# Fewer key loads per head, one load for the reciprocals, maxima written straight into the queries' rows, and other planned landing times

## Chip, core and metric

The kernel runs on one core of a Trainium2 chip. The time is that of one execution on the device in microseconds (us), lower is better. TensorE (PE) multiplies matrices, VectorE (DVE), ScalarE (ACT) and GpSimd (POOL) work elementwise, and SyncE (SP) issues all DMAs of this kernel, in the order of its program.

## What is computed

Two independent parts stand side by side in the output, 2048 rows of 2 x 448 columns, all in float32:

```
a = real part of a 2D discrete Fourier transform of A_x[2048, 448], by matrix products:
    y = Cr @ (x @ Wre^T) - Ci @ (x @ Wim^T)
qkv = B_x[2048, 448] @ wqkv[448, 1344]          # 16 heads, 28 wide
p = softmax(q @ k^T / sqrt(28))                 # per head 2048 x 2048
b = concat_heads(p @ v) @ wo[448, 448]
out = concat([a, b], axis=-1)
```

B_x, wqkv and wo are scaled up by 8, so that the scores are large and the maxima have to be subtracted before the exponential.

## The kernel before

**A planner writes the order.** Nothing in the program is scheduled on the chip: each engine runs its instructions in program order and waits on semaphores. The kernel first collects tasks (`pe`, `act`, `dve`, `pool`, `dma`), each with a key (when it is wanted), dependencies, buffers and a planned duration, and `Schedule.run` then plays an event simulation of its own: whenever an engine is free in the plan, it takes the ready task with the smallest key and emits its instructions. For a DMA the plan takes an issue time of about 0.38 us on SP and a landing time worked out from a size in KB and an `extra` in us; at most `LANES` = 8 DMAs are in flight, and a further one waits for the eighth before it. Where the chip is later than the plan, an engine stands at the early instruction, and all that is behind it in its queue stands too. Changing one planned number moves instructions on all engines.

**What TensorE runs.** Products of float32 precision are made of high and low parts in a rounded format (fp32r). First x @ wqkv: the projections of queries and keys (`project`, matmuls at L547) go to the DRAM tensor `qk_d`, two numbers (high, low) for each element, one row of 2048 columns per channel; the values (`values`) go to `v_d`. The Fourier part (`hidden` at L547, `sequence` at L662) is the filler: its keys are spread from the start to 1120, and it fills TensorE between the matmuls of attention.

**Attention.** A unit is a head h and a chunk c of 512 queries. 64 units run in two lanes side by side. In `unit_kept` (48 units, three a head) all scores of the chunk are made once (L803, 16 matmuls), copied to SBUF by ACT (L415), reduced to a running maximum `rm` on DVE (L813), whose transposes (L820, L829) give the maxima `nm` and `mb`; POOL or DVE subtract them (L846), ACT takes the exponential (L850), and the product with the values (L734) runs in groups of eight. In `unit_twice` (16 units, one a head) the scores are made twice: a first pass (L753) only for the maxima (L757, L761); the negated maxima are transposed (`max_rows`, L716), split into a high part (ACT, L765) and a low part (DVE, L766) and stored to the DRAM tensor `nm_d` (L769), and loaded from there into rows 84 and 85 of the queries' tile `q` (L770). There they meet two rows of ones below the keys (L374), so that the matmul of the second pass (L781, 86 rows) subtracts the maxima itself, and ACT takes the exponential straight from PSUM (L785). `due` holds the keys of both passes: the lane of `unit_twice` has a pace `P_R` of 60, its first pass starts at i x `P_R`, its second `ahead` = 1.08 paces later. So the second pass of head h - 2 ends a little after the first pass of head h is to start.

**Loads of a head.** `head_loads` takes one of the two key tiles `k` (84 rows x 2048) for a head: it becomes free when the second pass of the head before the last is done. It is filled by four pairs of DMAs, one pair for each 512 columns: `rows_of` loads the 28 high rows twice (L689, 56 rows) and the 28 low rows once (L690). A matmul waits only for the pair of its own columns (`got_k[h, c]`). The queries of a unit are loaded by the same helper (`load_q`), the values by one DMA (L706).

**Sums.** The values have a column of ones, so the product's row 28 is the sum of the exponentials. `out_of` handles the four chunks of a head together (for the last two heads: pairs of units, 4 groups of 2; 18 groups in all): a matmul folds the partial products (L865), ACT copies them to `osb` (L867), one DMA takes the rows of sums to a [128, 16] tile `sm` (L870), DVE takes the reciprocals (L871), one DMA stores them to DRAM (`rd`, L872), and a DMA for each of the units loads its row of 512 reciprocals to all 32 rows of the unit in `sbc` (L876, with a step of 0 in the source). POOL multiplies (L879), and a DMA for each unit stores 28 rows to `on_d` (L882). The last projection loads these rows (L939, L944), splits them (L956, L411) and multiplies by wo (L974).

Of the kernel before, what the change touches and what calls it, by code (L numbers as in the profile page):

```python
# [11 lines left out]
F32 = mybir.dt.float32  # L12
# [8 lines left out]
S = 2048  # L21
D = 448
H = 16
DH = 28
P = 128
NT = S // P
CH = 512
NC = S // CH
KR = 3 * DH
VW = 32  # L30
# [16 lines left out]
def f32(ap):  # L47
    return ap.bitcast(F32)
# [11 lines left out]
FIRST = {"PE": 1.4, "ACT": 2.0, "DVE": 2.0, "POOL": 5.0, "SP": 0.75}  # L60
FLOW_AT = 4.1
X_ROWS = 2.0
AHEAD = 0.15
PE_TURN = 0.22

# [251 lines left out]
def tile_kernel(ctx, tc, xa, wre, wim, wd, xb, wqkv, wo, out):  # L317
    nc = tc.nc
    ctx.enter_context(tc.manual_schedule(engines={ET.PE, ET.Activation, ET.DVE, ET.Pool, ET.SP}))
    dram = ctx.enter_context(tc.tile_pool(name="dram", bufs=1, space=DRAM))  # L320
# [11 lines left out]

    qk_d = dram.tile([2 * D, 2, S], F32R, name="qkd")
    v_d = dram.tile([H, P, NT * VW], F32, name="vd")
    nm_d = [dram.tile([2, CH], F32, name=f"nmd{u}") for u in range(H * NC)]
    r_d = [dram.tile([P, NT if h < H - 2 else NT // 2], F32, name=f"rd{h}") for h in range(H - 2 + NC)]
    y_d = [dram.tile([P, D], F32, name=f"yd{t}") for t in range(NT)]
    on_d = dram.tile([D, S], F32, name="ond")
# [56 lines left out]
    def dma(key, emit, size=256, extra=0.0, n=1, **kw):  # L395

        return sch.add({"SP": 0.4}, key, lambda e: emit(), dmas=[(size, extra)] * n, **kw)
# [24 lines left out]
    lane_r = [u for u in units if u[1] in TWICE[u[0]]]  # L422
    lane_k = [u for u in units if u[1] not in TWICE[u[0]]]
    P_R = (T_END - T_ATT) / (len(lane_r) + 1.5)
    P_K = (T_END - T_ATT) / (len(lane_k) + 1.5)
    due = {}
    for lane, per, ahead, part in ((lane_r, P_R, 1.08, 1.0), (lane_k, P_K, 1.8, 1.0)):
        for i, u in enumerate(lane):
            due[u] = (T_ATT + i * per, T_ATT + (i + ahead) * per, part * per / 16)
    head_due = [min(due[h, c][0] for c in range(NC)) for h in range(H)]  # L430
# [254 lines left out]
    def rows_of(dst, once, r0, c0, c1):  # L685

        src = bass.AP(tensor=qk_d.tensor, offset=qk_d.offset + r0 * 2 * S + c0,
                      ap=[[2 * S, DH], [0 if once else S, 2], [1, c1 - c0]])
        nc.sync.dma_start(f32(dst[:2 * DH, :]), f32(src))  # L689
        nc.sync.dma_start(f32(dst[2 * DH:KR, :]), f32(qk_d[r0:r0 + DH, once, c0:c1]))  # L690

    def rows_ready(h, c, at):
        r = h * 2 * DH + at
        return [t for j in range(r // P, (r + DH - 1) // P + 1) for t in qk_done[j, c]]

    KT, VT, Q = {}, {}, {}
    got_k, got_v = {}, {}

    def head_loads(h):
        k = KT[h] = kt_s.slot()  # L700
        for c in range(NC):
            got_k[h, c] = [dma(head_due[h] - 14 + c, lambda c=c: rows_of(
                k.t[:, c * CH:(c + 1) * CH], 1, h * 2 * DH + DH, c * CH, (c + 1) * CH),
                size=84, extra=X_ROWS, n=2, deps=rows_ready(h, c, DH), use=[k])]
        v = VT[h] = v_s.slot()
        got_v[h] = [dma(head_due_b[h] - 12, lambda: nc.sync.dma_start(  # L706
            v.t.rearrange("p c t d -> p (c t d)"), v_d[h]), deps=[d for c in range(NC) for d in v_done[c]], use=[v])]
# [34 lines left out]
    def unit_twice(u):  # L742
        h, c = u
        t_a, t_b, dt = due[u]
        q = qr_s.slot()
        lq = load_q(u, q)
        mx, nm = mx_s.slot(), nm_s.slot()
        ms = []
        for kc in range(NC):
            for qt in range(4):  # L750
                o = bank_s.slot()
                key = t_a + (kc * 4 + qt) * dt
                m = pe(key, lambda e, o=o, kc=kc, qt=qt: nc.tensor.matmul(  # L753
                    o.t, q.t[:KR, qt * P:(qt + 1) * P], KT[h].t[:KR, kc * CH:(kc + 1) * CH], start=True, stop=True),
                    deps=[*lq, *got_k[h, kc], before.get("ra")], use=[o, q, KT[h], mx])
                in_line("ra", m)
                ms.append(dve(key - 20, lambda o=o, kc=kc, qt=qt: nc.vector.tensor_reduce(  # L757
                    mx.t[:, qt, kc:kc + 1], o.t, axis=AX.X, op=ALU.max), deps=[m],
                    use=[o, mx]))
        key = t_a + 16 * dt - 20  # L760
        r = dve(key, lambda: nc.vector.tensor_reduce(nm.t, mx.t, axis=AX.X, op=ALU.max, negate=True), 0.2,  # L761
                deps=ms, acq=[nm], use=[mx])
        o, n2 = bank_s.slot(), n2_s.slot()
        t = max_rows(key, o, nm, r)
        a = act(key, lambda o=o: nc.scalar.activation(n2.t[:, 0, :], o.t[:4, :P], AF.Copy), 0.2, deps=[t], acq=[n2], use=[o])  # L765
        b = dve(key, lambda o=o: nc.vector.tensor_tensor(n2.t[:, 1, :], o.t[:4, :P], f32(n2.t[:, 0, :]), op=ALU.subtract), 0.25,  # L766
                deps=[a], use=[o, n2])
        nd = nm_d[h * NC + c]
        s = dma(key, lambda: nc.sync.dma_start(nd.rearrange("r (a b) -> a r b", a=4), f32(n2.t)), size=4, deps=[b], use=[n2])  # L769
        ld = dma(key, lambda: nc.sync.dma_start(f32(q.t)[KR:KR + 2, :], nd), size=4, deps=[s], use=[q])  # L770
        po = bank_s.slot()
        last_pv = None
        for g in range(NT // GV):
            tiles, es = [], []
            for kt in range(GV * g, GV * (g + 1)):
                o = bank_s.slot()
                if kt % 2 == 0:
                    tiles.append(kept_s.slot())
                p = Half(tiles[-1], kt % 2)
                key = t_b + kt * dt  # L780
                m = pe(key, lambda e, o=o, kt=kt: nc.tensor.matmul(  # L781
                    o.t, KT[h].t[:KR + 2, kt * P:(kt + 1) * P], q.t[:KR + 2, :], start=True, stop=True),
                    deps=[ld, before.get("rb")], use=[o, p.pair, q, KT[h], po])
                in_line("rb", m)
                es.append(act(key - 20, lambda o=o, p=p: nc.scalar.activation(p.t, o.t, AF.Exp, scale=SCALE),  # L785
                              deps=[m], use=[o, p.pair]))
            last_pv = pv_group(u, g, tiles, [*es, last_pv], po, key)
        unit_out(u, po, last_pv, key - 20)
# [67 lines left out]
    def out_of(us, rd):  # L856

        key = max(due[u][1] for u in us) + 10
        n = len(us)
        o, pair = bank_s.slot(), kept_s.slot()  # L860
        osb, sbc = Half(pair, 0), Half(pair, 1)

        def emit(e):
            for i, u in enumerate(us):
                nc.tensor.matmul(o.t[i * VW:(i + 1) * VW, :], fold, OU[u].t, start=True, stop=True)  # L865
        m = pe(key, emit, d=0.86, deps=[ou_done[u] for u in us], use=[o, *(OU[u] for u in us)], mode=1)
        a = act(key - 20, lambda: nc.scalar.activation(osb.t[:n * VW], o.t[:n * VW], AF.Copy), deps=[m], use=[o, pair])  # L867

        sm = sm_s.slot()
        s2 = dma(key, lambda: nc.sync.dma_start(sm.t[:, :n * NC], osb.t[DH:n * VW:VW, :]), 8, 0.7, deps=[a], use=[sm, pair])  # L870
        r = dve(key - 20, lambda: nc.vector.reciprocal(sm.t[:, :n * NC], sm.t[:, :n * NC]), 0.3, deps=[s2], use=[sm])  # L871
        s3 = dma(key, lambda: nc.sync.dma_start(rd, sm.t[:, :n * NC]), 8, deps=[r], use=[sm])  # L872

        def spread():
            for i in range(n):
                nc.sync.dma_start(sbc.t[i * VW:(i + 1) * VW, :], bass.AP(  # L876
                    tensor=rd.tensor, offset=rd.offset + i * CH, ap=[[0, VW], [1, CH]]))
        s4 = dma(key, spread, 64, n=n, deps=[s3], use=[pair])
        mul = pool(key - 20, lambda: nc.gpsimd.tensor_tensor(osb.t[:n * VW], osb.t[:n * VW], sbc.t[:n * VW], op=ALU.mult),  # L879
                   deps=[s4], use=[pair])  # L880
        for i, (h, c) in enumerate(us):
            o_done[h, c] = dma(key, lambda i=i, h=h, c=c: nc.sync.dma_start(  # L882
                on_d[h * DH:(h + 1) * DH, c * CH:(c + 1) * CH], osb.t[i * VW:i * VW + DH, :]), 56, deps=[mul], use=[pair])
# [21 lines left out]
    key = fkey(0, 0)  # L905
# [5 lines left out]
    key = fkey(0, 0)  # L911
# [19 lines left out]
    for n, c in enumerate(LAST):  # L931
        raws = []
        for k in range(4):
            pair = kept_s.slot()
            raw = Half(pair, 0)
            key = T_OUT + n
            deps = [o_done[h, c] for h in range(H) if (h + 1) * DH > k * P and h * DH < (k + 1) * P] + [before["ka"]]
            if k < 3:
                ld = dma(key, lambda raw=raw, k=k, c=c: nc.sync.dma_start(raw.t, on_d[k * P:(k + 1) * P, c * CH:(c + 1) * CH]),  # L939
                         deps=deps, use=[pair])  # L940
            else:
# [3 lines left out]
                ld = dma(key, twice, 128, n=2, deps=deps, use=[pair])  # L945
            raws.append((raw, ld))
        for i in range(2):
            x = kt_s.slot()
            ready = []
            for k in range(4):  # L950
                raw, ld = raws[k]
# [3 lines left out]
                key = T_OUT + n + i / 2  # L955
# [7 lines left out]
            for t in range(2):  # L963
# [12 lines left out]
                pair = kept_s.slot()  # L976
# [43 lines left out]
```

## Time and profile before

| | us |
|---|---|
| median of 3 runs | 1185.3 (1184.34 to 1186.82) |
| the profiled execution, its own time | 1186.24 |
| its span in the trace | 1184.5 |
| TensorE: time in L662 (big, whi), L803, L734, the costliest groups | 328.6, 292.0, 240.7 |
| POOL in the subtraction L846 | 626.9 |
| DVE in the running maximum L813 | 461.1 |
| ACT in copies L415 and exponentials L850 | 408.5, 395.1 |
| SP: wait for POOL at L515 (weight loads of the Fourier part), 77 times | 235.8 |

The granted TensorE clock is 0.997 of full speed over the span. The page of a profile gives each engine's busy time; idle time of an engine that isn't the bottleneck costs nothing by itself. Because matmuls overlap (one takes some 0.37 to 0.41 us and the next starts after 0.2), TensorE counts as busy through short waits. "Waited for" is told by the instruction that came last before the wait ended. SP's issues aren't counted as work of an engine, but they take time on SP: SPq is its queue. The prediction shows the lines that it reads.

### The profile page before, as it was taken

The numbers are of one execution on the slowest core, as the hardware profiler recorded it, in microseconds if no ns is written. First come the engines' busy times: TensorE is split into PE (matmuls) and PEld (weight loads), VectorE is DVE, ScalarE is ACT, GpSimd is POOL, SyncE is SP. The second block draws the span as 40 slices with busy tenths as digits, with TensorE's granted clock in tenths as the row PEclk, the third lists the DMA queues.
The fourth block names the chain that finished last, engine by engine and source line by source line (L and its number), as shares of the span: only waits on it lengthen the run. The fifth ranks groups of instructions, "written<-read, shape, count | busy, mean of one in ns | idle before, by whom it ended". The sixth has DMA issues, their size and how long they took to land.

```text
span 1184.5 us, 19835 instructions
## 1 busy us (share of the span) xinstructions
PE 1164.1 (98%) x6426; PEld 809.4 (68%) x6426; DVE 936.7 (79%) x1468; ACT 1056.5 (89%) x1777; POOL 909.9 (77%) x525
## 2 busy tenths in 40 slices
PE   8999999999999999999999999999999999999998
PEld 7876656666667666766666667666667676667677
DVE  6599988888888868877787888987877888877742
ACT  5279999999999989998899999999999999999942
POOL 1157868989888979877797989897987897997730
PEclk9999999999999999999999999999999999999999
DMA  7792235322323232323132232323232423223643
GB/s 244 165 225 107 100 124 174 90 81 62 106 68 110 62 109 67 105 72 90 62 102 89 78 118 67 106 64 111 83 99 89 121 76 115 87 62 100 188 130 119
DMA packets 111736, 125.18 MB, mean 106 GB/s; under 512 B 49264, under 2 KB 63216, under 8 KB 111632
## 3 DMA queue, kind: packets, MB, share of 16 engines
q1 hardware_dynamic: 111632, 123.91, 35.4%
q8 instruction: 51, 0.84, 0.3%
q14 instruction: 53, 0.43, 0.1%
HBM read 89.98 MB, written 33.75 MB: 104 GB/s over the span
## 4 chain that ended last, share of the span: by engine, by line
PE 82%; ACT 6%; DMA 4%; DVE 2%; issue 2%; POOL 2%; SPq 1%; ACTq 0%; POOLq 0%; DVEq 0%
PE bank L662 23%; PE bank L734 17%; PE bank L803 14%; PE bank L547 11%; PE bank L781 5%; PE bank L753 5%; PE bank L974 3%; ACT kept L415 3%; PE bank L820 2%; PE bank L829 2%; DVE rm L813 2%; ACT kept L850 1%; PE bank L865 1%; DMA kept<-xb 1%; POOL kept L846 1%
## 5 line engine op out<-in xcount | busy, mean ns | idle before, releaser
L846 POOL TENSOR_TENSOR kept<-kept,mb 128x1024 f32<-128x1024 f32 x263 | 626.9, 2404 | 124.0 <-ACT mb L831 101.4
L813 DVE TENSOR_TENSOR rm<-bank,rm 128x512 f32<-128x512 f32 x672 | 461.1, 686 | 74.9 <-ACT kept L415 33.5
L415 ACT ACTIVATE kept<-bank 128x512 f32<-128x512 f32 (+1 forms) x715 | 408.5, 633 | 53.9 <-PE bank L803 34.6
L850 ACT ACTIVATE kept<-kept 128x1024 f32<-128x1024 f32 x372 | 395.1, 1102 | 11.3 <-DVE kept L846 5.5
L662 PE MATMUL bank<-big,whi 128*128 128x448 f32 x1024 | 328.6, 370 | 0.0
L803 PE MATMUL bank<-qk,k 84*128 84x512 f32 x768 | 292.0, 410 | 2.7 <-ACT kept L415 1.4
L522 POOL TENSOR_TENSOR wlo<-wraw,whi 128x512 fp32r<-128x512 f32 (+1 forms) x166 | 204.0, 1232 | 70.3 <-ACT whi L516 46.7
L734 PE MATMUL bank<-kept,v 128*32 128x512 f32 x1988 | 240.7, 597 | 0.7 <-DVE rm L813 0.5
L662 PEld LDWEIGHTS bank<-big,whi 128*128 128x128 f32 x1024 | 193.7, 190 | 28.8 <-issue 3.5
L803 PEld LDWEIGHTS bank<-qk,k 84*128 84x128 f32 x768 | 141.9, 189 | 69.3 <-DVE rm L813 17.7
L662 PE MATMUL bank<-big,wlo 128*128 128x448 f32 x512 | 189.0, 369 | 0.0
L757 DVE TENSOR_REDUCE mx<-bank 128x1 f32<-128x512 f32 x256 | 173.3, 682 | 18.8 <-PE bank L753 18.0
L785 ACT ACTIVATE kept<-bank 128x512 f32<-128x512 f32 x250 | 157.6, 639 | 5.3 <-PE bank L781 5.0
L734 PEld LDWEIGHTS bank<-kept,v 128*32 128x32 f32 x1988 | 56.6, 109 | 124.0 <-issue 111.9
L846 DVE TENSOR_TENSOR kept<-kept,bank 128x1024 f32<-128x1024 f32 x109 | 131.8, 1212 | 2.6 <-ACT mb L831 2.4
L516 ACT ACTIVATE whi<-wraw 128x512 fp32r<-128x512 f32 x167 | 112.1, 673 | 17.0 <-DMA wraw<-wqkv 12.2
L781 PE MATMUL bank<-qr,k 86*128 86x512 f32 x256 | 104.3, 411 | 2.9 <-DMA qr<-nmd 2.2
L662 PEld LDWEIGHTS bank<-big,wlo 128*128 128x128 f32 x512 | 97.2, 190 | 13.7 <-issue 0.8
L753 PE MATMUL bank<-k,qr 84*128 84x512 f32 x256 | 103.5, 413 | 2.3 <-ACT kept L785 0.9
L547 PE MATMUL bank<-wd,whi 128*128 128x448 f32 x256 | 80.6, 368 | 0.1
L547 PE MATMUL bank<-big,whi 128*128 128x512 f32 x196 | 69.8, 400 | 2.0 <-ACT big L482 0.9
L822 DVE TENSOR_REDUCE nm<-bank 128x4 f32<-128x512 f32 x48 | 33.1, 690 | 46.5 <-PE bank L820 43.4
(80 smaller groups left out, 1062.0 us busy)
## 6 DMA issues: line engine op xcount, KB each, us to landing
wraw<-wre SPq DMA_DIRECT2D x64, 256.0 KB
wraw<-wim SPq DMA_DIRECT2D x64, 256.0 KB
qkd<-wd SPq DMA_DIRECT2D x32, 256.0 KB
wraw<-xa SPq DMA_DIRECT2D x32, 256.0 KB
k<-qkd SPq DMA_DIRECT2D x64, 112.0 KB
out<-kept SPq DMA_DIRECT2D x32, 224.0 KB
qkd<-kept SPq DMA_DIRECT2D x24, 256.0 KB
qk<-qkd SPq DMA_DIRECT2D x48, 112.0 KB
```

The lines of the kernel that those rows point to most:

```text
L415: nc.scalar.activation(dst, src, AF.Copy)
L522: b = sch.add(e, at, lambda g: eng[g].tensor_tensor(self.lo.t[:, :n], raw.t[:, :n], f32(self.hi.t)[:, :n], op=ALU.subtract), deps=[a], acq ...
L547: nc.tensor.matmul(o.t[:, :cols], w(), x(), start=(i == 0), stop=(i == n - 1))
L662: nc.tensor.matmul(o.t[:, :D], a.t[:, k, :], b[:, q * 4 + k, :], start=(q == 0 and k == 0 and j == 0), stop=(q == 3 and k == 3 and j == 2))
L734: nc.tensor.matmul(o.t[j * VW:(j + 1) * VW, :], VT[h].t[:, kt // 4, j, :], pairs[i // 2].t[:, i % 2, :], start=(kt < 4), stop=(kt >= NT - 4))
L753: m = pe(key, lambda e, o=o, kc=kc, qt=qt: nc.tensor.matmul(o.t, q.t[:KR, qt * P:(qt + 1) * P], KT[h].t[:KR, kc * CH:(kc + 1) * CH], start ...
L757: ms.append(dve(key - 20, lambda o=o, kc=kc, qt=qt: nc.vector.tensor_reduce(mx.t[:, qt, kc:kc + 1], o.t, axis=AX.X, op=ALU.max), deps=[m], ...
L781: m = pe(key, lambda e, o=o, kt=kt: nc.tensor.matmul(o.t, KT[h].t[:KR + 2, kt * P:(kt + 1) * P], q.t[:KR + 2, :], start=True, stop=True), ...
L803: m = pe(key, lambda e, o=o, kt=kt: nc.tensor.matmul(o.t, KT[h].t[:KR, kt * P:(kt + 1) * P], q.t[:KR, :], start=True, stop=True), deps=[*l ...
L813: prev = dve(key - 20, lambda o=o: nc.vector.tensor_tensor(rm.t, o.t, rm.t, op=ALU.max), deps=[m, prev], use=[rm, o], lock=[o], own=RAW)
L846: eng[e].tensor_tensor(s.t, s.t, over_pair(pm.t if e == "DVE" else mb.t), op=ALU.add)
L850: es.append(act(key, lambda s=s: nc.scalar.activation(s.t, s.t, AF.Exp, scale=SCALE), 0.96, deps=[sh], use=[s]))
```

## The change

1. A head's keys are loaded by one pair of DMAs for all 2048 columns, for heads 1 to 15; head 0 keeps its four pairs. All four `got_k[h, c]` are this one load, which waits until all four chunks of the projection are stored. Its planned `size` is 344 and its `extra` `X_K` = 2.0, for each of the two DMAs.
2. The negated maxima no longer go through DRAM (`nm_d` is gone): two DMAs, one for each of the high and low parts, take the [4, 128] values from `n2` to one row of 512 in the queries' tile. Planned `extra` `X_NM` = 0.3.
3. The reciprocals of a group are loaded by one DMA to all n x 32 rows (source: n chunks, each row 32 times by a step of 0, 512 columns), in place of n DMAs.
4. Planned landings in `out_of`: the sums' load has an `extra` of 3.0 in place of 0.7, the store and the load of the reciprocals 1.5 in place of 0.
5. `ahead` of the `unit_twice` lane is 1.04 in place of 1.08.

```diff
+X_K = 2.0
+X_NM = 0.3
...
-    nm_d = [dram.tile([2, CH], F32, name=f"nmd{u}") for u in range(H * NC)]
...
-    for lane, per, ahead, part in ((lane_r, P_R, 1.08, 1.0), (lane_k, P_K, 1.8, 1.0)):
+    for lane, per, ahead, part in ((lane_r, P_R, 1.04, 1.0), (lane_k, P_K, 1.8, 1.0)):
...
-        for c in range(NC):
-            got_k[h, c] = [dma(head_due[h] - 14 + c, lambda c=c: rows_of(
-                k.t[:, c * CH:(c + 1) * CH], 1, h * 2 * DH + DH, c * CH, (c + 1) * CH),
-                size=84, extra=X_ROWS, n=2, deps=rows_ready(h, c, DH), use=[k])]
+        if h == 0:
+            for c in range(NC):
+                got_k[h, c] = [dma(head_due[h] - 14 + c, lambda c=c: rows_of(
+                    k.t[:, c * CH:(c + 1) * CH], 1, h * 2 * DH + DH, c * CH, (c + 1) * CH),
+                    size=84, extra=X_ROWS, n=2, deps=rows_ready(h, c, DH), use=[k])]
+        else:
+            ld = dma(head_due[h] - 14, lambda: rows_of(k.t, 1, h * 2 * DH + DH, 0, S), size=344, extra=X_K, n=2,
+                     deps=[t for c in range(NC) for t in rows_ready(h, c, DH)], use=[k])
+            for c in range(NC):
+                got_k[h, c] = [ld]
...
-        nd = nm_d[h * NC + c]
-        s = dma(key, lambda: nc.sync.dma_start(nd.rearrange("r (a b) -> a r b", a=4), f32(n2.t)), size=4, deps=[b], use=[n2])
-        ld = dma(key, lambda: nc.sync.dma_start(f32(q.t)[KR:KR + 2, :], nd), size=4, deps=[s], use=[q])
+        def put():
+            for r in range(2):
+                nc.sync.dma_start(f32(q.t)[KR + r:KR + r + 1, :].rearrange("r (a b) -> r a b", a=4), f32(n2.t)[:, r, :])
+        ld = dma(key, put, size=2, extra=X_NM, n=2, deps=[b], use=[n2, q])
...
-        s2 = dma(key, lambda: nc.sync.dma_start(sm.t[:, :n * NC], osb.t[DH:n * VW:VW, :]), 8, 0.7, deps=[a], use=[sm, pair])
+        s2 = dma(key, lambda: nc.sync.dma_start(sm.t[:, :n * NC], osb.t[DH:n * VW:VW, :]), 8, 3.0, deps=[a], use=[sm, pair])
...
-        s3 = dma(key, lambda: nc.sync.dma_start(rd, sm.t[:, :n * NC]), 8, deps=[r], use=[sm])
-
-        def spread():
-            for i in range(n):
-                nc.sync.dma_start(sbc.t[i * VW:(i + 1) * VW, :], bass.AP(
-                    tensor=rd.tensor, offset=rd.offset + i * CH, ap=[[0, VW], [1, CH]]))
-        s4 = dma(key, spread, 64, n=n, deps=[s3], use=[pair])
+        s3 = dma(key, lambda: nc.sync.dma_start(rd, sm.t[:, :n * NC]), 8, 1.5, deps=[r], use=[sm])
+
+        s4 = dma(key, lambda: nc.sync.dma_start(sbc.t[:n * VW, :], bass.AP(
+            tensor=rd.tensor, offset=rd.offset, ap=[[CH, n], [0, VW], [1, CH]])), 64 * n, 1.5, deps=[s3], use=[pair])
```

## The prediction

> **What bounds the kernel now.** First the page's busy times, and the same for the middle stage (its length, then each engine's busy time and count, TensorE first).
>
> ```profile
> span 1184.5 us, 19835 instructions
> PE 1164.1 (98%) x6426; PEld 809.4 (68%) x6426; DVE 936.7 (79%) x1468; ACT 1056.5 (89%) x1777; POOL 909.9 (77%) x525
> ...
> 40.00:1085.00 1045.00, 1034.38 (x5777) 708.10 (x5780) 864.21 (x1343) 977.76 (x1639) 861.30 (x482) 1.00 0.33 98
> ```
>
> TensorE sets the end: it idles 20.4 us of 1184.5, of which 10.6 between 40 and 1085 us; the rest is the start, where nothing has landed yet, and the end, after the last matmul. The change gives TensorE the same matmuls (5329 in either program). So what it can win lies in the 10.6 us of the middle, plus whatever short waits overlapping matmuls hide. Second view: what TensorE waited for (in total, times, longest).
>
> ```profile
> PE bank L781 <- DMA qr<-nmd: 2.2, 3, 0.8
> PE bank L829 <- DVE nm L822: 1.9, 1, 1.9
> PE bank L753 <- ACT kept L785: 0.9, 1, 0.9
> PE bank L803 <- ACT ou L415: 0.8, 1, 0.8
> PE bank L753 <- DVE rm L813: 0.7, 1, 0.7
> PE bank L753 <- DMA qr<-qkd: 0.6, 1, 0.6
> ```
>
> These six rows are 7.1 of the 10.6 us. Each wait was followed in the timeline and the chain of waits to what was late first.
>
> **The negated maxima.** A row of the timeline, and then the chain of waits up to 417.61 us (start, duration, what):
>
> ```profile
> 410.99 0.27 PE L716 MATMUL bank<-ident,nm 128*4 128x128 f32 x1
> ```
>
> ```profile
> 411.57 0.83 SPq L689
> ...
> 414.55 1.58 DMA nmd<-n
> ...
> 416.14 1.43 DMA qr<-nmd
> ...
> 417.61 0.50 PE bank L781
> ```
>
> The maxima's first load could go only after SP had issued the key loads (L689, L690) ahead of it; then two DMAs ran one after the other, 1.58 + 1.43 = 3.0 us, and SP stood still between them. After the change two DMAs of one half each go straight into the queries' rows, neither waiting for the other. L770's issue takes 0.23 us:
>
> ```profile
> L770 SPq DMA_DIRECT2D qr<-nmd x16: 222/226/252, 105.0 to 1049.9; - x16
> ```
>
> So the chain is 0.23 + about 1.5 = 1.8 us in place of 3.0. Bounds: below, the single 1.43; above, if on-chip writes of 512 bytes took as long as both today, 3.0. I take 1.8, for each half is no larger than nmd's DMA was. That is 1.2 us less, and each of the three waits of L781 was at most 0.8. In the changed order, 23 to 89 instructions of TensorE stand between the transpose of the maxima and the first matmul of the second pass (21 for the first unit, as before): 5 us or more of cover, where the chain from transpose to matmul now needs about 6.6 (410.99 to 417.61) less 1.2 and less the queue of key loads. The 2.2 us go. The second pass is also planned earlier (1.04 for 1.08 of the lane's pace); that spends part of the cover and is inside those counts.
>
> **The sums.** The timeline around 552 us (start, duration, engine, line; in brackets idle time before and who ended it):
>
> ```profile
> 550.13 0.39 SPq L690 DMA_DIRECT2D qr<-qkd  x1
> ...
> 552.48 0.93 PE L753 MATMUL bank<-k,qr 84*128 84x512 f32 x3 [0.65 <-DMA qr<-qkd]
> 552.50 0.61 SPq L870 DMA_DIRECT2D sm<-kept  x1
> ...
> 555.07 0.25 DVE L871 RECIPROCAL sm<-sm 128x16 f32<-128x16 f32 x1 [4.13 <-DMA sm<-kept]
> ...
> 555.92 0.65 PE L829 MATMUL bank<-ident,nm 128*128 128x128 f32 x4 [1.91 <-DVE nm L822]
> ```
>
> The reciprocal (L871) stood in VectorE's queue too early: the sums' load was issued at 552.50, late behind the key loads, and landed 2.57 us later, and VectorE's whole queue, the maxima of L822 included, waited 4.13 us. TensorE paid 1.91. The 0.7 of L753 behind L813 is the same, with the reciprocal waiting right before L813:
>
> ```profile
> 426.39 0.25 DVE L871 RECIPROCAL sm<-sm 128x16 f32<-128x16 f32 x1 [1.25 <-DMA sm<-kept]
> ...
> 427.24 0.50 PE L753 MATMUL bank<-k,qr 84*128 84x512 f32 x1 [0.70 <-DVE rm L813]
> ```
>
> The change puts 2.3 us more into the planned landing of this load, so other VectorE work stands ahead of L871. Its cost is nothing, as long as the maxima and shifts that take its place are ready; if they aren't, VectorE idles as now. What is late instead is the reciprocal itself, by about 2 us, and behind it one multiply on POOL and a store whose reader is the last projection, hundreds of us later for all but the last four. Gain 1.9 + 0.7 = 2.6.
>
> The reciprocals' way back, in the chain of waits:
>
> ```profile
> 624.94 2.17 DMA kept<-rd
> ...
> 629.77 2.41 POOL kept L846
> ...
> 633.80 0.73 PE bank L803 x2
> ```
>
> And how long POOL and VectorE waited in all, with the issue times (minimum, median, maximum in ns):
>
> ```profile
> POOL kept L879 <- DMA kept<-rd: 23.1, 9, 8.9
> DVE sm L871 <- DMA sm<-kept: 7.2, 5, 4.1
> L876 SPq DMA_DIRECT2D kept<-rd x64: 302/413/1499, 177.6 to 1149.8; - x64
> ```
>
> POOL waits at L879 for the copies of the reciprocals; of the 23.1 us only one case reached TensorE, by way of L846, the exponentials and the 0.8 of "ACT ou". Now four issues of 0.41 become one, 1.2 us of SP less, and the landing is planned 1.5 us later for L872 and for L876. One load of 256 KB: below, 2.17 as the last of today's four. Above, if it ran on a quarter of the DMA engines: the queue's 123.91 MB over 35.4% of 16 engines' span (row below) are 18.5 GB/s an engine, so 64 KB an engine take 3.5 us where 16 KB take 0.9, and 2.17 becomes 4.8. The plan gives it 4.4. I take 3.5, between the ends. Either end leaves POOL waiting under a microsecond or not at all, where it waits some 2.5 today, so the 0.8 goes.
>
> The Trainium skill, "DMA: Bandwidth & Descriptors", "Rules for kernel authors", speaks against this edit: the slowest dimension of an access pattern sets how many DMA engines a transfer uses, and an outer dimension of 4 confines it to 4. The new source has the 4 heads' chunks outermost (2 for the last four groups). By that rule the load takes the upper value, about 4.8 us, and POOL would wait some 0.4 us; the sum would not change by more than the 0.8. No run before shows such a load's engines.
>
> **The keys.** Fifteen of sixteen heads load their keys by 2 DMAs in place of 8:
>
> ```profile
> q1 hardware_dynamic: 111632, 123.91, 35.4%
> ...
> k<-qkd SPq DMA_DIRECT2D x64, 112.0 KB
> ...
> k<-qkd SPq DMA_DIRECT2D x64, 56.0 KB
> ...
> L689 SPq DMA_DIRECT2D k<-qkd x64: 797/812/2307, 21.3 to 994.2; - x64
> L690 SPq DMA_DIRECT2D k<-qkd x64: 333/547/1111, 22.4 to 995.0; - x64
> ```
>
> Four pairs take 4 x (0.81 + 0.55) = 5.4 us of SP, one pair 1.4: 4 us fewer in which queries, sums and weights stand behind them. That releases the 0.6 of "DMA qr<-qkd", issued at 550.13 among the key loads, and the 0.9 of L753 at 687 us, where a weight load behind them came late:
>
> ```profile
> 681.20 0.55 SPq L690 DMA_DIRECT2D k<-qkd  x1
> ...
> 681.85 2.91 DMA wraw<-wd
> ...
> 687.33 0.50 PE L753 MATMUL bank<-k,qr 84*128 84x512 f32 x1 [0.85 <-ACT kept L785]
> ```
>
> The price: the first product of a head now waits for all 672 KB, not the first 168. The keys' buffer is released by the second pass of the head before the last, right before the new head's first pass, so this is nearly on the path. From release: 0.9 to the second issue, then 2.35 as from 550.13 to 552.48, then 504 KB more at 16 x 18.5 GB/s, 1.7 us: 5.0 in all. Above, if issue time grew with bytes (0.81 to 3.2), 7.3; below, with 84 rows and no growth by bytes, 3.3. I take 5.0, for the number of rows stays. In the changed order 28 to 43 instructions of TensorE stand between release and first use (33 to 48 before). By these rows of the chain one takes 0.21 (L662) or 0.23 (L803):
>
> ```profile
> 619.85 0.62 PE bank L662 x3
> 620.47 0.23 PE bank L803
> ```
>
> That is 6.4 to 9.0 us of cover, six of the fourteen under 6.6. Held, by a bit over a microsecond. Cost 0, with up to 6 us at the upper bound (the eight covers shorter than 7.3).
>
> **The sum.** 2.2 + 1.9 + 0.7 + 0.8 + 0.6 + 0.9 = 7.1 us of named waits. The new plan reorders every engine, so it draws chance waits of its own; I let a third of the 7.1 come back, 2.3, a choice and not a measurement. Net 4.8. The profiled execution is 1186.24 with a span of 1184.5 (1.7 around it) and would be 1181.4; it lies 0.9 above the median of 1185.3, so the median becomes 1180.5.
>
> **Rivals.** (a) More: POOL, VectorE and SP also lose waits that TensorE feels only as short gaps inside its busy time; if all 10.6 us of the middle go, 1185.3 - 10.6 = 1174.7. For it: 23.1 us of POOL and 7.2 of VectorE go; against: the larger POOL waits come from L831, which the change doesn't touch. (b) Nothing: the removed waits were the plan's chance meetings, and the new order has as many; 10.6 us stay, 1185. For it: only 3 of 16 units waited for their maxima; against: the causes above are systematic, landings later than planned. (c) Slower: a head's keys land later than their cover. From 7.2 us after the release on, the shortfalls of the short covers eat the gain; at 8 us they sum to 13.0 over the fourteen heads, 1185.3 - 4.8 + 13.0 = 1193.5. For it: 256 KB weight loads share the engines, 0.9 us each; against: the 5.0 worked out. (d) The edit of the reciprocals' load doesn't shorten anything (four engines): that leaves forecast and time as they are, within 0.8.
>
> **How the numbers follow.** Forecast (1177 to 1183, with (d)) 0.50; (a) 0.12; (b) 0.16; (c) 0.22. A measurement here can't tell less than about 0.2%, 2.4 us, from no change. Faster, under 1182.9: 0.12 and nearly all of 0.50, 0.61; same 0.17; slower 0.22. Range 1174 to 1192: from (a) to most of (c).
>
> **What would show it.** Right: no wait of L781 for qr; L871 without idle time before it; POOL's wait for kept<-rd at the multiply (L879 before) well under 23.1 us; 38 issues of k in place of 128 (4 chunks of head 0 and 15 whole heads, two each); idle TensorE between 40 and 1085 us near 6. Wrong: L753 waiting for k<-qkd at the head changes, or new waits behind ACT or POOL that sum to more than 7 us; a tail after the last attention matmul longer than today's.

## The result and the profile after

| | before | changed |
|---|---|---|
| median of 11 runs, us | 1185.0 (1183.34 to 1187.1) | 1192.08 (1188.2 to 1196.18) |
| ratio to before, 95% interval | | 1.0058 [1.0042, 1.0075] |
| span of the profiled execution, us | 1184.5 | 1193.8 |

The change made the kernel 7 us slower; 1180.5 was forecast. The changed kernel's busy times and the same middle stage (its length, then TensorE's busy time and how many of its records fall in it, and so on):

```profile
span 1193.8 us, 19637 instructions
PE 1166.8 (98%) x6426; PEld 809.3 (68%) x6426; DVE 933.2 (78%) x1471; ACT 1055.0 (88%) x1773; POOL 911.8 (76%) x526
...
40.00:1085.00 1045.00, 1028.64 (x5730) 701.59 (x5732) 853.02 (x1332) 966.35 (x1619) 858.63 (x480) 1.00 0.34 97
```

In the middle stage TensorE now idles 1045.0 - 1028.6 = 16.4 us, 10.6 before, and got through 5730 matmul records, 5777 before. What waited for what (in total, times, longest): three of TensorE's rows in the middle stage, the two largest among them, then GpSimd's wait at the multiply by the reciprocals and SP's wait to store its result.

```profile
PE bank L760 <- DMA qr<-qkd: 7.0, 6, 1.6
...
PE bank L811 <- ACT kept L793: 2.5, 2, 2.0
...
PE bank L663 <- POOL wlo L523: 1.1, 1, 1.1
...
POOL kept L884 <- DMA kept<-rd: 34.7, 13, 5.7
...
SPq L887 <- POOL kept L884: 62.6, 18, 5.8
```

GpSimd's was 23.1 us before; SP's in the kernel before was this:

```profile
SPq L882 <- POOL kept L879: 32.8, 17, 3.2
```

In the changed kernel's line numbers L760 is the first pass (L753 before), L884 the multiply (L879), L887 its store (L882). Neither the wait for the maxima (2.2 before) nor the one behind the reciprocal's VectorE instruction (1.9) is among TensorE's waits any more: these two went as forecast. Two larger causes of waiting took their place, the queries' load at the head changes and the reciprocals' load.

**At a head change.** Timeline of the changed kernel (start, duration, engine, line), then one row of its chain of waits:

```profile
864.47 0.40 PE L789 MATMUL bank<-qr,k 86*128 86x512 f32 x1
...
864.90 0.87 SPq L690 DMA_DIRECT2D k<-qkd  x1
...
865.82 0.54 SPq L691 DMA_DIRECT2D k<-qkd  x1
...
866.42 0.37 SPq L690 DMA_DIRECT2D qr<-qkd  x1
...
872.96 0.48 PE L760 MATMUL bank<-k,qr 84*128 84x512 f32 x1 [1.64 <-DMA qr<-qkd]
```

```profile
866.83 5.99 DMA qr<-qkd
```

The key loads take hardly longer to issue than a quarter of a head did (0.87 and 0.54, where the medians before were 0.81 and 0.55). But the queries' load issued right behind them landed 5.99 us after 866.83, where the one at 550.13 in the kernel before, among the four pairs, took 2.35. There SP had sent the queries before the last quarter of the keys.

**At a group's sums.** Timeline around 690 us:

```profile
687.39 0.56 SPq L882 DMA_DIRECT2D kept<-rd  x1
...
688.05 0.89 SPq L516 DMA_DIRECT2D wraw<-xa  x2
...
693.83 1.27 POOL L884 TENSOR_TENSOR kept<-kept 128x512 f32<-128x512 f32 x1 [3.06 <-DMA kept<-rd]
694.15 0.63 ACT L517 ACTIVATE whi<-wraw 128x512 fp32r<-128x512 f32 x1 [2.64 <-DMA wraw<-xa]
...
695.32 0.99 PE L811 MATMUL bank<-qk,k 84*128 84x512 f32 x2 [1.98 <-ACT kept L793]
```

The one load of the reciprocals is issued at 687.39 and lets GpSimd go on only at 693.83, 6.4 us later; the weight load issued right behind it at 688.05 also lands about 6.1 us later. ScalarE waits 2.64 for that load in its queue, the exponentials behind it are late, and TensorE pays 1.98. In the 13 cases where GpSimd waited for this load, it went on 4.9 to 6.4 us after the load's issue began.

### The profile page after: what moved, and what is told of

The parts are those of the page before. It is cut to its first block, busy times and chain, and to the rows that moved or that the text cites. A ratio compares the mean times of both kernels' runs of the same rounds, so it can differ in the third digit from the quotient of the medians.

```text
span 1193.8 us, 19637 instructions
## 1 busy us (share of the span) xinstructions
PE 1166.8 (98%) x6426; PEld 809.3 (68%) x6426; DVE 933.2 (78%) x1471; ACT 1055.0 (88%) x1773; POOL 911.8 (76%) x526
## 4 chain that ended last, share of the span: by engine, by line
PE 81%; ACT 6%; DMA 5%; issue 2%; POOL 2%; DVE 2%; SPq 1%; DVEq 0%; ACTq 0%; POOLq 0%
PE bank L663 25%; PE bank L741 15%; PE bank L811 14%; PE bank L548 10%; PE bank L760 5%; PE bank L789 5%; PE bank L979 3%; DMA qr<-qkd 3%; ACT kept L416 2%; PE bank L828 2%; POOL kept L854 2%; ACT kept L858 2%; PE bank L837 2%; DVE rm L821 1%; DMA kept<-xb 1%
## 5 line engine op out<-in xcount | busy, mean ns | idle before, releaser
L854 POOL TENSOR_TENSOR kept<-kept,mb 128x1024 f32<-128x1024 f32 x269 | 641.7, 2409 | 109.5 <-ACT mb L839 100.5
L416 ACT ACTIVATE kept<-bank 128x512 f32<-128x512 f32 (+1 forms) x722 | 421.3, 641 | 57.5 <-PE bank L811 36.4
L858 ACT ACTIVATE kept<-kept 128x1024 f32<-128x1024 f32 x377 | 403.0, 1110 | 13.4 <-POOL kept L854 9.6
L663 PE MATMUL bank<-big,whi 128*128 128x448 f32 x1024 | 323.6, 369 | 0.0
L811 PE MATMUL bank<-qk,k 84*128 84x512 f32 x768 | 287.2, 410 | 4.0 <-ACT kept L793 2.5
L741 PE MATMUL bank<-kept,v 128*32 128x512 f32 x1980 | 244.4, 603 | 0.1
L793 ACT ACTIVATE kept<-bank 128x512 f32<-128x512 f32 x236 | 151.9, 653 | 12.3 <-PE bank L789 12.0
L517 ACT ACTIVATE whi<-wraw 128x512 fp32r<-128x512 f32 x167 | 114.6, 686 | 15.9 <-DMA wraw<-wqkv 9.1
L760 PE MATMUL bank<-k,qr 84*128 84x512 f32 x256 | 103.5, 410 | 10.4 <-DMA qr<-qkd 7.0
L663 PEld LDWEIGHTS bank<-big,wlo 128*128 128x128 f32 x512 | 96.8, 189 | 17.4 <-issue 3.4
L789 PE MATMUL bank<-qr,k 86*128 86x512 f32 x256 | 103.1, 412 | 0.3 <-ACT kept L793 0.3
```

What stands on the lines that cost most here:

```text
L416: nc.scalar.activation(dst, src, AF.Copy)
L663: nc.tensor.matmul(o.t[:, :D], a.t[:, k, :], b[:, q * 4 + k, :], start=(q == 0 and k == 0 and j == 0), stop=(q == 3 and k == 3 and j == 2))
L741: nc.tensor.matmul(o.t[j * VW:(j + 1) * VW, :], VT[h].t[:, kt // 4, j, :], pairs[i // 2].t[:, i % 2, :], start=(kt < 4), stop=(kt >= NT - 4))
L760: m = pe(key, lambda e, o=o, kc=kc, qt=qt: nc.tensor.matmul(o.t, q.t[:KR, qt * P:(qt + 1) * P], KT[h].t[:KR, kc * CH:(kc + 1) * CH], start ...
L789: m = pe(key, lambda e, o=o, kt=kt: nc.tensor.matmul(o.t, KT[h].t[:KR + 2, kt * P:(kt + 1) * P], q.t[:KR + 2, :], start=True, stop=True), ...
L811: m = pe(key, lambda e, o=o, kt=kt: nc.tensor.matmul(o.t, KT[h].t[:KR, kt * P:(kt + 1) * P], q.t[:KR, :], start=True, stop=True), deps=[*l ...
```

## The experiments

The kernel before ran beside each of them (medians 1184.4 to 1184.6 in the three sets). Idle TensorE is 1045.0 less its busy time between 40 and 1085 us in the profiled execution.

| run | what | median us | ratio to before, 95% | TensorE idle, us |
|---|---|---|---|---|
| changed | all five parts | 1192.1 | 1.0058 [1.0042, 1.0075] | 16.4 |
| e1 | changed, keys in four pairs | 1187.4 | 1.0030 [1.0014, 1.0047] | 14.1 |
| e2 | changed, reciprocals in n loads | 1182.2 | 0.9972 [0.9958, 0.9987] | 10.0 |
| e3 | changed, keys planned 2 us later | 1188.1 | 1.0026 [1.0010, 1.0043] | 7.9 |
| e4 | before, keys in one pair | 1193.7 | 1.0066 [1.0040, 1.0092] | 13.1 |
| e5 | changed, source pattern 128 outermost | 1181.7 | 0.9987 [0.9968, 1.0005] | 8.3 |
| e6 | before, reciprocals in one load | 1207.5 | 1.0210 [1.0188, 1.0232] | 21.5 |
| e7 | changed, keys in four, reciprocals in n | 1174.0 | 0.9930 [0.9904, 0.9956] | 7.1 |
| e8 | changed, reciprocals in n, keys planned 2 us later | 1173.8 | 0.9924 [0.9901, 0.9946] | 2.7 |
| e9 | changed, reciprocals planned 2.5 us later | 1185.6 | 1.0010 [0.9999, 1.0022] | 9.8 |
| e10 | before, sums planned later | 1175.0 | 0.9923 [0.9905, 0.9941] | 3.7 |
| e11 | before, maxima straight to the queries | 1179.4 | 0.9962 [0.9949, 0.9974] | 8.5 |
| e12 | as e2, queries issued ahead of keys | 1183.1 | 0.9985 [0.9970, 0.9999] | 10.1 |

**e1: keys in four pairs again, the rest as changed.**

```diff
-        if h == 0:
+        if True:
             for c in range(NC):
                 got_k[h, c] = ...
```

> The changed kernel (median 1192.1), with the keys of every head in four pairs of loads again and all else as changed. Theory K (the one pair of loads for a whole head is the cause: the queries of the two-pass unit are issued right behind it and land some 5 to 6 us later than the order of TensorE allows): the first pass no longer waits for the queries' load (7.0 us in the changed kernel, under 1.5 here), and the median falls by 5 to 8 us, to 1184 to 1187. Rival R (the one load of the reciprocals is the cause, through GpSimd and through the loads queued behind it): 1190 to 1193, GpSimd's wait for that load stays near 35 us. Rival C (the new order as a whole, chance waits): anywhere, with waits of TensorE for other things than these two.

Measured: 1187.4, 4.7 us less than the changed kernel, just above theory K's range. The wait of the first pass for the queries' load is gone from TensorE's waits, but GpSimd still waits 35.7 us for kept<-rd. So the keys cost something here, and are not all of it: theory K alone falls short.

**e2: reciprocals in n loads again, the rest as changed.**

```diff
-        s4 = dma(key, <one load of n * VW rows>, 64 * n, 1.5, deps=[s3], use=[pair])
+        s4 = dma(key, spread, 64, 1.5, n=n, deps=[s3], use=[pair])
```

> The changed kernel with the reciprocals in one load for each unit again (planned 1.5 later, as changed), keys still in one pair. Theory K: 1189 to 1193, the first pass still waits about 7 us for the queries' load; GpSimd's wait for the reciprocals falls from 35 us to under 15. Rival R: 1184 to 1187.

Measured: 1182.2, 9.9 less than the changed kernel and 2.3 less than the kernel before. That was below even what the rival R expected, and outside theory K. The waits of this kernel for the reciprocals and for the queries' load:

```profile
POOL kept L887 <- DMA kept<-rd: 4.9, 3, 2.1
...
SPq L890 <- POOL kept L887: 23.3, 15, 3.6
...
PE bank L760 <- DMA qr<-qkd: 4.4, 5, 1.3
```

34.7 became 4.9 and 62.6 became 23.3. The queries still come late (4.4), so two costs lie side by side.

**e3: the key loads planned 2 us later.**

```diff
-X_K = 2.0
+X_K = 4.0
```

> The changed kernel with one number of the plan changed: the key loads' planned landing 2 us later (4.0 in place of 2.0 for X_K); the same DMAs. Theory K in the form that the plan believes an early landing: other matmuls of TensorE stand before the head's first pass, its wait for the queries falls under 2.5 us, and the median to 1185 to 1188. Theory K in the form that the load itself costs (the DMA engines, not the place in the order): 1190 or more. Rival R: 1190 to 1193.

Measured: 1188.1, 4.0 less than the changed kernel, just above the range of the first form of theory K, with the same DMAs. No wait for qr<-qkd is left among TensorE's waits. What the whole-head load costs is mostly its planned place: told the truth about the landing, the plan puts other matmuls ahead of the first pass.

**e4: the kernel before, with keys in one pair.**

```diff
+X_K = 2.0
...
-        for c in range(NC):
-            got_k[h, c] = [dma(head_due[h] - 14 + c, ...
+        if h == 0: ...
+        else:
+            ld = dma(head_due[h] - 14, lambda: rows_of(k.t, 1, h * 2 * DH + DH, 0, S), size=344, extra=X_K, n=2, ...
```

> The kernel before (median 1185.0) with the keys of heads 1 to 15 in one pair of loads, nothing else of the change. Theory K: the wait for the queries' load appears (0.6 us before, 3 to 8 here), 1188 to 1193. Rival R: 1183 to 1187.

Measured: 1193.7, 9.3 more, a little over the range; the wait for the queries is 2.9 us in 6 waits, just under its range. That wait alone doesn't make 9.3. Idle TensorE rose by 2.5, and the mean time lost to the clock by 2.6 (last section); the rest is not shown by any row here, and the run's order differs from before everywhere.

**e5: the same load with 128 outermost.** Every instruction stands where it stands in the changed kernel; only the source's access pattern differs.

```diff
-            tensor=rd.tensor, offset=rd.offset, ap=[[CH, n], [0, VW], [1, CH]])), ...
+            tensor=rd.tensor, offset=rd.offset, ap=[[0, n * VW], [1, CH]])), ...
```

> The changed kernel in every instruction and its order, but the source of the one reciprocals' load is read with an outermost dimension of 128 (64 for the last four) and a step of 0, in place of 4 (2): the same 256 KB in one DMA. It leaves out the reciprocals of all units but the first of a group, whose values go to all rows. Theory D (the outer dimension of 4 confines the load to 4 DMA engines, it lands late and holds up loads queued behind it): GpSimd's wait for kept<-rd falls from 34.7 us to under 10, SP's wait for the multiply from 62.6 to under 35, and the median from 1192.1 to 1182 to 1186. Rival (one DMA of 256 KB is slow however it is laid out, or its planned place is wrong): 1190 to 1194.

Measured: 1181.7, 10.4 less than the changed kernel and a little under theory D's range; GpSimd's wait (10.9) and SP's (35.0) fell almost as far as it said. Timeline of the same group as above, then the waits:

```profile
680.87 0.33 SPq L882 DMA_DIRECT2D kept<-rd  x1
681.30 0.85 SPq L516 DMA_DIRECT2D wraw<-xa  x2
...
684.90 1.30 POOL L884 TENSOR_TENSOR kept<-kept 128x512 f32<-128x512 f32 x1 [0.63 <-DMA kept<-rd]
685.41 0.63 ACT L517 ACTIVATE whi<-wraw 128x512 fp32r<-128x512 f32 x1 [0.43 <-DMA wraw<-xa]
```

```profile
POOL kept L884 <- DMA kept<-rd: 10.9, 8, 3.4
...
SPq L887 <- POOL kept L884: 35.0, 16, 5.9
```

From issue to multiply 4.0 us in place of 6.4, and the weight load behind it 4.1 in place of 6.1. One DMA of 256 KB is thus not slow as such; with an outermost dimension of 4 in its source it is. The start times and durations of the single packets in the two traces show why. Where the load ran alone in the changed kernel (issued at 500.19), its 128 packets of 2048 bytes ran mostly four at a time, and the last ended 4.65 us after the issue began. In e5 (issued at 620.94) they ran mostly seven to nine at a time, and the last ended after 2.76 us. A packet took 84 ns in median in both, so it is not the repeated reading of one row that makes e5's load fast. With an outermost dimension of 2 (the last four groups) two ran at a time (issued at 1158.24). Around 694 us, after GpSimd had gone on, the loads issued behind the reciprocals also finished four packets at a time. The rule of the Trainium skill that the prediction weighed ("DMA: Bandwidth & Descriptors", "Rules for kernel authors") agrees with this; which engines carried a packet is not in the traces.

**e6: the kernel before, with the reciprocals in one load.**

```diff
-        s4 = dma(key, spread, 64, n=n, deps=[s3], use=[pair])
+        s4 = dma(key, <one load, ap=[[CH, n], [0, VW], [1, CH]]>, 64 * n, deps=[s3], use=[pair])
```

> The kernel before with the reciprocals in the one load of the change (outer dimension 4), and nothing else of the change. Theory D: GpSimd's wait for kept<-rd rises from 23 to 35 us or more, and the median from 1184.4 to 1188 to 1193. Rival (it costs only together with the other parts): 1183 to 1187.

Measured: 1207.5, 23 more, far beyond the range that theory D gave. Here the plan still believes an early landing:

```profile
POOL kept L876 <- DMA kept<-rd: 44.6, 9, 10.6
...
SPq L879 <- POOL kept L876: 77.6, 18, 5.6
```

It is the costliest single part. Inside the change it cost about 10; that the later planned landings hid the rest fits e9, but was not tried on this kernel. The time lost to the clock is also 5.4 larger than before there (last section), so part of the 23 may lie in it.

**e7: neither of the two.** The edits of e1 and e2 together.

> The changed kernel without its parts on the keys and on the reciprocals' load: maxima straight into the queries' rows, sums planned later and the second pass planned earlier stay. Theory K+D (both costs are real and add): 1176 to 1180, under the 1182.2 with the keys in one pair. If the pair of key loads costs nothing once the other load is mended: 1181 to 1184.

Measured: 1174.0, 18.1 less than the changed kernel and 0.7% [0.44, 0.96] faster than before, 2 us under the range of theory K+D. Both costs are real, and together they are more than the sum of the two alone (4.7 and 9.9). Against e2 the key loads cost 8.2, against e1 the reciprocals' load costs 13.4.

**e8: reciprocals in n loads, the keys in one pair and planned 2 us later.** The edits of e2 and e3 together.

> The changed kernel with the reciprocals in n loads and the key loads' landing planned 2 us later (X_K 4.0). Theory K (the key load is planned to land too early): the wait of the first pass for the queries (4.4 us with X_K 2.0) falls under 1.5, the median to 1176 to 1180. Rival (order luck outweighs it): 1181 to 1186.

Measured: 1173.8, 2 us under theory K's range and faster than before by 0.76% [0.54, 0.99]. No wait for qr<-qkd is left among TensorE's waits. TensorE's middle stage:

```profile
40.00:1085.00 1045.00, 1042.30 (x5852) 717.42 (x5850) 876.33 (x1364) 988.26 (x1657) 870.88 (x489) 1.00 0.35 99
```

2.7 us idle, and 5852 records done by 1085 us. So the whole-head key load costs nothing measurable against four pairs (e7), once it is planned to land when it lands.

**e9: the one load of the reciprocals planned 2.5 us later.**

```diff
-            ... ap=[[CH, n], [0, VW], [1, CH]])), 64 * n, 1.5, deps=[s3], use=[pair])
+            ... ap=[[CH, n], [0, VW], [1, CH]])), 64 * n, 4.0, deps=[s3], use=[pair])
```

> The changed kernel with one number of the plan changed: the one load of the reciprocals is planned to land 2.5 us later (4.0 in place of 1.5); the same DMAs on the same engines. Theory D1 (what costs is that GpSimd's multiply and SP's store stand too early and wait): GpSimd's wait for kept<-rd falls from 34.7 us to under 10, SP's wait for the multiply under 35, and the median to 1181 to 1186. Theory D2 (what costs is that four DMA engines are held and weight or key loads queued behind land late): those waits fall as well, but the median stays at 1188 or more.

Measured: 1185.6, 6.4 less than the changed kernel.

```profile
PE bank L760 <- DMA qr<-qkd: 8.7, 9, 1.6
...
POOL kept L884 <- DMA kept<-rd: 12.4, 5, 6.0
...
SPq L887 <- POOL kept L884: 46.6, 15, 7.5
```

Neither theory is met in full: the waits fell, though not to 10 and 35, and the median lies at the upper edge of D1. About 6 of the 10 us of this part went with the load's planned place, which fits the queues of GpSimd and SP standing behind a load that was planned too early. The other 4 remain with the slow load (e5 against e9); the queries' wait is larger here than in e5 (5.7) and e2 (4.4), which would fit loads held up on the DMA side, but no run separates that from the order.

**e10: the kernel before, sums planned later.**

```diff
-        s2 = dma(..., 8, 0.7, deps=[a], use=[sm, pair])
+        s2 = dma(..., 8, 3.0, deps=[a], use=[sm, pair])
-        s3 = dma(..., 8, deps=[r], use=[sm])
+        s3 = dma(..., 8, 1.5, deps=[r], use=[sm])
-        s4 = dma(key, spread, 64, n=n, deps=[s3], use=[pair])
+        s4 = dma(key, spread, 64, 1.5, n=n, deps=[s3], use=[pair])
```

> The kernel before with only the planned landings of the change (sums 3.0, store and loads of the reciprocals 1.5 each). As the prediction had it: VectorE no longer waits for the sums (7.2 us before), GpSimd's wait for kept<-rd falls from 23.1 us to under 10, and the median falls by 3 to 5 us, to 1180 to 1182. If the plan's lateness costs nothing: 1183 to 1186.

Measured: 1175.0, 9.6 less, two to three times the expectation, from three numbers of the plan and not one changed instruction but their order.

```profile
40.00:1085.00 1045.00, 1041.26 (x5842) 717.48 (x5841) 873.33 (x1357) 985.89 (x1651) 864.09 (x485) 1.00 0.32 98
...
DVE sm L871 <- DMA sm<-kept: 2.3, 2, 1.2
...
POOL kept L879 <- DMA kept<-rd: 5.7, 3, 3.3
```

TensorE's idle fell by 6.9 (10.6 to 3.7), two thirds of what the middle stage had, GpSimd's wait at the multiply from 23.1 to 5.7 and VectorE's from 7.2 to 2.3.

**e11: the kernel before, maxima straight into the queries' rows.**

```diff
-        s = dma(key, <n2 to nd>, size=4, deps=[b], use=[n2])
-        ld = dma(key, <nd to rows 84, 85 of q>, size=4, deps=[s], use=[q])
+        ld = dma(key, put, size=2, extra=X_NM, n=2, deps=[b], use=[n2, q])
```

> The kernel before with only the maxima written straight into the queries' rows. As the prediction had it: 2 us less, 1181 to 1184, with no wait of the second pass over 1 us for the maxima. If chance order outweighs it: 1184 to 1188.

Measured: 1179.4, 5.2 less where 2 were expected, with 0.2 us of wait for the maxima left on TensorE. In the kernel before, SP itself stood at the maxima's second load until the first had landed, a wait that can't occur here:

```profile
SPq L770 <- DMA nmd<-n: 18.3, 16, 2.1
```

The prediction named this standstill and gave it no price. That it makes the other 3 us is not shown: GpSimd's wait for the reciprocals also fell, to 11.3, in the new order.

**e12: queries ahead of the keys.** On top of the edit of e2:

```diff
+        first = c in TWICE[h] and h > 0
-        return [dma(due[u][0] - 12, lambda: rows_of(q.t, 0, ...
+        return [dma(head_due[h] - 15 if first else due[u][0] - 12, lambda: rows_of(q.t, 0, ...
```

> The changed kernel with the reciprocals in n loads, and the queries of the two-pass unit issued ahead of its head's key loads (key of head_due - 15). Theory K with the queue as its place (the queries land late because they stand behind 672 KB of keys): the first pass waits under 2 us in all for the loads (4.4 in the kernel with n loads and the keys first), 1176 to 1180. If the keys themselves land too late: the wait goes over to the keys' load, 4 us or more, 1180 to 1184.

Measured: 1183.1, as e2 (1182.2) and inside the second range, though the wait for the keys is 2.0 and not 4. The wait for the queries is gone and others stand in its place:

```profile
PE bank L790 <- DMA qr<-n: 2.4, 3, 1.3
PE bank L761 <- DMA k<-qkd: 2.0, 4, 1.0
PE bank L812 <- DVE rm L822: 1.8, 2, 1.4
```

The first pass now waits for the keys themselves (L761). So the queries' place in the queue was not the root: the keys, too, land later than the plan believes, which e3 and e8 mend and this doesn't.

## Why the prediction was wrong

- **What bounds the kernel.** TensorE, and what can be lost or won lies in the middle stage: right. That no more than 10.6 us can be won there: right in size, in part by luck (the best run wins 10.6, but only 7.9 of it is idle time of the middle stage; the mean time lost to the clock is about 2 less).
- **The maxima.** Right in kind: L789 (the second pass) doesn't wait for them in the changed kernel. Alone they gave 5.2 where the sum had 2.2; SP's standstill at L770 (18.3 us) was left without a price. The issue was mis-sized the other way: 0.61 us in median for each of the two (L777), where the sum had 0.23 in all.
- **The sums planned later.** Right in kind, too small by two thirds: 2.6 for VectorE and 0.8 for GpSimd were counted from the named waits of TensorE, and e10 gave 9.6. The few waits of TensorE that could be traced back to late landings were too small a measure of their cost; GpSimd's wait fell by 17.4 there and VectorE's by 4.9, but which of them makes the difference is not shown.
- **The reciprocals' load: the step that failed.** "Either end leaves POOL waiting under a microsecond or not at all, where it waits some 2.5 today, so the 0.8 goes", and rival (d) "within 0.8". The upper bound of 4.8 was about right for the load alone (4.65), but in the 13 cases where GpSimd waited the multiply came 4.9 to 6.4 us after the issue began, and GpSimd's wait rose to 34.7. The part costs about 10 us inside the change (e2, e5) and 23 alone (e6). Two things were left out of the step: the loads that SP issues right behind it, which land late too, and SP itself, which stands at the store until the multiply is done (62.6 us). The rule that spoke against the edit was read, its landing worked out, and then priced by GpSimd's wait alone.
- **The keys.** "5.0 in all" from release to landing, covered by 6.4 to 9.0. Measured: 8.1 us from the end of the last second-pass matmul (864.47 + 0.40) to the first product at 872.96, and 7.0 us in six waits. Two terms were too small. The data of the last three quarters was to take 1.7 us, which would have ended the load at about 869.9; the last of the keys' 84 packets in this head ended at 871.67. And the queries behind the keys were forgotten in the step: the first product needs them too, and they landed at 872.83. Rival (c) named this mechanism and a time of 1193.5, near what came by luck: it had 13.0 us for the keys alone, which cost 4.7 (e1) to 8.2 (e7 against e2), and the larger half was the reciprocals.
- **The allowance** of 2.3 us for chance waits can't be judged from these runs. The second pass planned earlier (1.04 for 1.08) was not tried alone, so what it is worth stays open.

The parts don't add: alone, four of the five measure +9.3 (e4), +23.0 (e6), -9.6 (e10) and -5.2 (e11), a sum of +17.6 where the whole change shows +7.1. It fits that the later landings of part 4 already hide much of what part 3 costs (planning part 3's load 2.5 us later still took off another 6.4 in e9), but no run shows it directly.

## What to carry to other kernels

Before coalescing DMAs, look at the outermost dimension of the access pattern (4 here), and at what the issuing queue sends right behind: a load that holds up its followers is priced by them, not by its own reader. Where queues run in a planned order, compare each planned landing with the measured one first; correcting three numbers here (e10) was worth more than any saved DMA did alone. A whole-tile load in place of pieces also takes away the early first piece, so its planned place must move with it (e3, e8).

## What the runs showed of the hardware

The granted clock goes with much of the scatter between runs of one kernel. A straight line of time against the time lost to the clock, (1 - granted clock) x time, has a slope of 1.0 over the 25 runs of the kernel before in the first set, 0.8 over the 13 of the second and 0.6 over the 21 of the third; a slope of 1 would mean that each microsecond lost there is one in the result. The mean loss is 2.8 us before, 3.8 in the changed kernel, 5.4 in e4, 8.2 in e6 and 0.6 in e8. It does not simply follow TensorE's idle time: e1 (14.1 us idle) lost 1.9, e3 (7.9) lost 4.6. In the traces the clock stands at half for spells of about 3.4 us or twice that, three inside the changed kernel's work and two inside the kernel before's. Of the 16 spells in all traces between 40 us and the last matmul, 12 began within 4.5 us of the start of an idle gap of TensorE of about 1 us or more (1.91 us for the one at 557 us in the kernel before), and 4 did not. What starts a spell was not tried.

Larger contiguous rows were not faster here: in the changed kernel's trace the 8192-byte packets (the key rows, with some 60 of another queue) took 542 ns in median, the 2048-byte ones 84, so four of these take 336. The two kinds also differ in what they load; no run changes the packet size alone.
